# The order of short and long products on TensorE: an FNet transform ahead of a squared-ReLU layer

## The chip, the cores and the metric

The kernel runs on one core of one Trainium2 chip. The metric is the device time of one execution in microseconds, as the median of several runs.

## The reference

The input x has 8 sequences of 3008 tokens with 256 features. Each sequence goes through a two-dimensional Fourier transform, of which the real part is kept; the 24064 resulting rows go through two dense products with a squared ReLU between them.

```
X = np.fft.fft(x, axis=1)
X = np.fft.fft(X, axis=2)
x = X.real.reshape(B * S, D)        # 8 * 3008 rows, D = 256
h = x @ w_in                        # 256 -> 2048
r = np.maximum(h, 0.0)
out = (r * r) @ w_out               # 2048 -> 256
```

All is float32.

## The kernel before

**The parts.** The transform over the features is folded into w_in ahead of time (tables G1 and G2). What is left for each sequence b is a real cosine and sine transform over the tokens, in two tiles Pt and Qt for each sequence. They are made by symmetries: the rows of x are folded into sums and differences, split by even and odd frequency (kp = 0 and 1) and by cosine and sine (which = 0 and 1), so that only short products with the tables cosT and sinT remain. The highest feature of all later sequences is a case of its own, the "lone column": dft_ops(None), whose weights are 7 columns wide (one for each of the sequences 1 to 7) and not 128.

**The main loop.** The outer loop runs over steps i, each a sequence b, a block of token frequencies k0 of 252 columns (246 columns in some blocks) and a pair j of chunks of the hidden layer. In one step, TensorE (PE) does the following, in the order in which it is written:

1. `front`: four products into hP (G1 by Pt) and hQ (G2 by Qt), at line 1040. VectorE (DVE) turns them into g: two `he` instructions at line 1044 read hP, then lines 1048 and 1049 read hQ and `he`.
2. Products with w_out or with sums of its parts (wsum), for a pair of steps whose g is complete, in `run` at line 1105. They come from a fast matrix scheme: `first_half` has 12 products into the banks F, `second_half` has 8 into the banks S. Odd i has the F half, even i has the S half.

ScalarE (ACT) then does relu and square on g (lines 1053 and 1056), and GpSimd (POOL) makes the sums s of them (lines 1068 to 1085) that later products with w_out read.

**The transform beside it.** While the loop works on one sequence, the transform of the next one is laid into it piece by piece. The folding is DVE, ACT and POOL work, done by `pieces` and `first_pieces`. The products of the transform are in the two functions `even` and `odd` of each of four groups (kp, which). `even` has a product of class 0, one of class 1 (line 769) and two of `once_more` (line 867). `odd` has four of `twice_more` (line 893). These are the short products: 94 or 95 columns stream, where a product with w_out streams 164 or 168. After its four products, each function issues copies out of the bank pd on ACT (oc at lines 872 and 897, da at line 788) and then the joins on DVE (lines 804 to 821 and 905 to 929), which write Pt or Qt at the end. These functions are called through a hook: `run` calls it between two of the products with w_out. Which step gets which function is planned by `pace`, `spent` and `share`; at most one such function goes into one step.

**Banks.** hP, hQ and pd come from one pool, psh, with two buffers of the tag "h", taken in turn. In a step with a hook, hP and hQ take the two buffers and pd takes the one that hP had. The next step's hP takes that of hQ, and its hQ takes that of pd. Each instruction waits by semaphore for the last user of the buffer that it takes.

Each engine issues in the order written; tc.manual_schedule() leaves that order alone. A float32 product is two instructions on PE (two passes), and each has a weight load (PEld) of its own.

Of the kernel before, what the change touches and what calls it, by code (L numbers as in the profile page):

```python
# [84 lines left out]
def kernel(  # L85
# [111 lines left out]
    def part_of(tab, t):  # L197
        return tab[t in LATE]
# [542 lines left out]
    def dft_ops(b):  # L741
# [8 lines left out]
        def group(kp, which):  # L750
            both_in = b == 0 and which == 1
            n = NE if b is None else P
            tab = sinT if which == 1 else cosT
            n2, _, n1, n0 = NC[kp]
            st = {}

            def product(ps, c, lone_e=False, only=None):

                ts = [t for t in range(NT) if TILES[t][0] == c]
                for t in ts if only is None else ts[only:only + 1]:  # L760
                    rows = TILES[t][3]
                    if b is None:
                        w = we[0:rows, SPOT[t], kp]
                    elif lone_e:
                        w = lone[0:rows, 2 * t + kp]
                    else:
                        w = folded[b, t][0:rows, kp, PART[which]]
                        w = w[:, 0:n - both_in]
                    nc.tensor.matmul(ps[0:w.shape[-1]], w,  # L769
                                     part_of(cosT if lone_e else tab, t)[0:rows, kp, PLACE[t]:PLACE[t] + NC[kp][c]],  # L770
                                     start=t == ts[0] and (lone_e or not both_in), stop=t == ts[-1] and not lone_e,
                                     skip_group_check=both_in)
# [4 lines left out]
            def even_n():  # L777
                st["ps"] = psh.tile([P, 512], F32, name="pd", tag="h")[0:n]
                for c, at, nk in EVEN:
                    if b != 0 and c == 2:  # L780
                        st["half"] = once_more(st["ps"][:, at:], nk)
                    else:
                        product(st["ps"][:, at:at + nk], c)
                copy_4()

            def copy_4():
                a = st["a"] = hp.tile([P, -(-n2 // 16) * 16], F32, name="da", tag="da", bufs=2)[0:n]
                nc.scalar.copy(a[:, 0:n2], st["ps"][0:n, 0:n2])
# [67 lines left out]
            def once_more(ps, nk):  # L856

                nq = (nk + 2) // 2 if kp else (nk + 1) // 2
                pair = TWO, TWO + 1
                for part in range(2):  # L860
                    if kp:
                        tab, o = (cosT, sinT)[part], 0
                        to = ps[:, part * nq:part * nq + nq]
                    else:
                        tab, o = (cosT, sinT)[which], part
                        to = ps[:, part:nk:2]
                    nc.tensor.matmul(to, left(pair[part != which]),  # L867
                                     columns(tab, TWO, o)[0:HALF2], start=True, stop=True)
                if not kp:
                    return ps[:, 0:nk]  # L870
                a = hp.tile([P, NC[0][3] // 2 + 9], F32, name="oc", tag="oc", bufs=1)[0:n, 0:nq]
                nc.scalar.copy(a, ps[:, 0:nq])
                return a, ps[:, nq:2 * nq]

            def twice_more(ps):

                av, aw, bv, bw = (left(ODD0 + i) for i in range(4))  # L880
                if kp:
                    nq = (n0 + 2) // 2
                    spots = [(tab, part, ps[:, i * nq + part:(i + 1) * nq:2])
                             for i, tab in enumerate((cosT, sinT)) for part in range(2)]
                    ws = (aw, bw, bv, av) if which else (av, bv, bw, aw)
                else:
                    tab = (cosT, sinT)[which]
                    spots = [(tab, 0, ps[:, 0:n0:4]), (tab, 1, ps[:, 2:n0:4]),
                             (cosT, 0, ps[:, 1:n0 + 1:4]), (sinT, 0, ps[:, 3:n0:4])]
                    ws = (bw, aw, bv, av) if which else (av, bv, aw, bw)  # L890
                for (tab, part, to), w in zip(spots, ws):
                    cols = quarters(tab, part)
                    nc.tensor.matmul(to, w, cols[:, cols.shape[-1] - to.shape[-1]:],  # L893
                                     start=True, stop=True)
                ps_a = ps[:, 0:nq] if kp else ps[:, 5:n0 + 1:4]
                a = hp.tile([P, NC[0][3] // 2 + 9], F32, name="oc", tag="oc", bufs=1)[0:n, 0:ps_a.shape[-1]]
                nc.scalar.copy(a, ps_a)
                if kp:
                    return a, ps[:, nq:2 * nq]
                st["turned"] = a, ps_a, ps[:, 3:n0:4]  # L900
                return ps[:, 0:n0]
# [9 lines left out]
            def odd_n():  # L911
                ps = psh.tile([P, 512], F32, name="pd", tag="h")[0:n]
                st["odd"] = ps[:, 0:n0]
                st["bankodd"] = ps, 0
                st["odd"] = twice_more(ps)

            def join_odd(what, nk):

# [26 lines left out]
            if b == 0:  # L945
                named = [("copy", copy_4), ("join_4", join_4), ("join_2", join_2), ("lo", lambda: join_lo(0, NK1)),
                         ("keep", keep), ("rest", lambda: join_lo(NK1, n0)), ("hi", join_hi)]
                for e in range(2):
                    for t in range(NT):
                        c = TILES[t][0]  # L950
                        f = odd_part if c == 3 else even_part
# [1 line left out]
                        named.append((("", "e")[e] + str(t), lambda f=f, args=args: f(*args)))  # L953
                return [((which, kp, nm), f) for nm, f in named]
            def even():
                even_n()
                if kp:
                    st["bankhalf"] = st["ps"], 2 * n2
                    join_odd("half", n1)
                join_4()  # L960
                join_2()

            def odd():
                odd_n()
                if kp:
                    join_odd("odd", n0)
                else:
                    join_turned()
                join_1()
# [127 lines left out]
    def run(products, q, n, hook, end=PAIRS):  # L1097

        tb = 2 * n // 3
        begun = set()  # L1100
        for k, (nm, slot, w, v) in enumerate(products):
            if hook and k == hook[0]:
                hook[1]()
            w = wsum[:, w, q] if isinstance(w, int) else A(*w)[:, q]
            nc.tensor.matmul(acc[nm][:, slot, 0:tb], w, v, start=q == 0 and nm not in begun, stop=q == end - 1,  # L1105
                             skip_group_check=True)
            begun.add(nm)
# [176 lines left out]
    def ahead(b):  # L1284
        (_, start), *groups = dft_ops(b)
        one, two = fold_later(b)
        if b > 1:
            return one + two + [(0.0, start)] + groups
        start()
        tables = {k: (lambda tab=tab, t=t: part_table(tab, t),)  # L1290
                  for k, (tab, t) in zip((13, 14, 15, 16), ((tab, t) for t in (TWO, ODD0) for tab in (cosT, sinT)))}
        extra.update({PLAIN + 1: (take_turn, make_turn), **tables, 17: (scale_turn,),
                      **fold_columns()})
        e, (n0, m0, n1, m1, store_e) = groups[0::2], dft_ops(None)
        ready = len(one)
        composites.extend([(ready, 0, e[0]), (ready, 0, e[1]), (0, 26, n0), (0, 26, m0), (0, 26, n1), (ready, 0, e[2]),
                           (0, 26, (m1[0], lambda: (m1[1](), store_e[1]()))), (ready, 0, e[3]),
                           *((len(one + two), 0, o) for o in groups[1::2])])
        return one + two

# [121 lines left out]
    def first_pieces(i, j):  # L1422


        nonlocal drawn
        room = CAPACITY[j]
        after, since, (_, f) = composites[0] if composites else (0, per, (0.0, None))
        if drawn >= after and i >= since and (j % 2 == 0 or not side):
            composites.pop(0)
            return 2, f  # L1430
        while side and side[0][0] <= room + 0.2:
            t, f = side.pop(0)
            f()
            drawn, room = drawn + 1, room - t

    def piece_beside():

        nonlocal spent
        if side and side[0][1] in beside and spent + side[0][0] / 2 <= 0:
            t, f = side.pop(0)  # L1440
            f()
            spent += t

    ROUNDED = ['3', 'w0', '4', 'w1', '5', 'w2', '6', 'w3', '7', 'w4', 'w5', 'w6', 'w7']
    PHASES = ('TS', 'PW', 'H', 'PR', 'PU', 'PL')
# [123 lines left out]
    i = 0  # L1569
# [17 lines left out]
    for i in range(PLAIN, len(steps) + 2):  # L1587
        if i < len(steps):
            b, k0, n, j = steps[i]
# [15 lines left out]
        hook = None  # L1605
        if i < len(steps) and share(i):
            spent -= pace * share(i)
            if i < per:
                hook = first_pieces(i, j)
            else:  # L1610
                pieces()
                hook = (2, piece_beside)
        while finished and finished[0][0] <= i:
            store(*finished.pop(0)[1:])
        group = (i - 3) // 2
        at, last_half = 2 * group, i % 2 == 0
# [103 lines left out]
```

## Time and profile before

| | |
|---|---|
| median of 3 runs | 1860.83 us (1860.78 to 1861.01) |
| the profiled execution | 1860.65 us, of which the span of instructions is 1858.6 |
| PE | busy 1850.1 us, 100% of the span, 11360 passes |
| PEld | busy 1748.1 us, 94%, 11360 loads |
| DVE | busy 1474.3 us, 79% |
| POOL | busy 1461.2 us, 79% |
| ACT | busy 1075.2 us, 58% |
| mean granted TensorE clock | 1.000 |

PE and PEld are the two halves of TensorE: PE streams columns through the array, PEld loads the weights of the next pass meanwhile. The time of a pass is read from the distance of two starts; the duration that is given for one includes the way through the array, and the durations of neighbouring passes overlap. A line of the timeline gives the start, the time to the end of the last of its instructions, the engine, the line of the program, the operation, what is written and read, the shapes, how many instructions are merged in it, and in brackets the idle time before it with what ended it. A row of the list of waits reads: who waited, for whom, microseconds in total, how many times, the longest.

### The profile page before, as it was taken

What the parts mean: (1) busy time and instruction counts of PE and PEld (TensorE: products, weight loads), DVE (VectorE), ACT (ScalarE), POOL (GpSimd) and SP (SyncE); (2) the same over time, 40 slices, a digit from 0 to 9 for tenths busy, and PEclk for the clock granted to TensorE, in tenths of its full rate; (3) what the DMA queues carried; (4) which work ended last, traced back from release to release, by engine and by line L of the source; (5) the groups of instructions that cost most, each with busy time, mean ns of one, the idle gap of its engine ahead of it and who ended that gap; (6) DMA issues with size and microseconds to landing.
All of it is one profiled execution on the core that took longest, in us unless ns stands there. A gap on an engine that the chain in (4) does not pass through costs nothing.

```text
span 1858.6 us, 33954 instructions
## 1 busy us (share of the span) xinstructions
PE 1850.1 (100%) x11360; PEld 1748.1 (94%) x11360; DVE 1474.3 (79%) x3472; ACT 1075.2 (58%) x1594; POOL 1461.2 (79%) x2137
## 2 busy tenths in 40 slices
PE   9999999999999999999999999999999999999999
PEld 7699999999999999999999999999999999999998
DVE  8998878887788878778788787788878887757666
ACT  5776546565555655656456564565645666444454
POOL 4499778788788887888778887788877878787885
PEclk9999999999999999999999999999999999999999
DMA  7441101111111101111011100111001100000010
GB/s 211 109 61 41 21 21 51 41 29 23 29 34 45 26 22 32 33 46 30 15 32 46 49 15 15 46 46 35 15 21 44 37 15 21 17 21 15 21 43 23
DMA packets 153265, 69.51 MB, mean 37 GB/s; under 512 B 132577, under 2 KB 144325, under 8 KB 153092
## 3 DMA queue, kind: packets, MB, share of 16 engines
q1 hardware_dynamic: 152546, 66.80, 14.6%
q8 instruction: 91, 1.49, 0.3%
q14 instruction: 82, 0.67, 0.1%
q0 software_dynamic: 416, 0.43, 0.1%
q10 hardware_dynamic: 130, 0.12, 0.0%
HBM read 42.60 MB, written 24.69 MB: 36 GB/s over the span
## 4 chain that ended last, share of the span: by engine, by line
PE 94%; DVE 2%; POOL 1%; ACT 1%; issue 0%; DMA 0%; SPq 0%; POOLq 0%; DVEq 0%; ACTq 0%
PE F L1105 34%; PE S L1105 23%; PE hQ L1040 17%; PE hP L1040 17%; PE pd L893 1%; PE pd L867 1%; PE pd L769 1%; PE pg L351 0%; PE fin L1214 0%; DVE fd L320 0%; DVE he L1026 0%; DVE wsum L420 0%; DVE g L1029 0%; ACT g L1053 0%; PE ph L1013 0%
## 5 line engine op out<-in xcount | busy, mean ns | idle before, releaser
L1053 ACT ACTIVATE g<-g 128x1008 f32<-128x1008 f32 (+1 forms) x384 | 399.4, 1040 | 307.3 <-DVE g L1049 282.1
L1044 DVE SCALAR_TENSOR_TENSOR he<-ew,gE,hP 128x252 f32<-128x252 f32 (+1 forms) x748 | 321.2, 471 | 284.1 <-PE hP L1040 284.1
L1056 ACT ACTIVATE g<-g 128x1008 f32<-128x1008 f32 (+1 forms) x384 | 399.4, 1040 | 12.0
L1040 PE MATMUL hQ<-Qt,G 128*128 128x252 f32 (+3 forms) x1496 | 379.3, 376 | 0.6 <-ACT g L1053 0.5
L1040 PE MATMUL hP<-Pt,G 128*128 128x252 f32 (+1 forms) x1496 | 378.9, 376 | 0.0
L1105 PE MATMUL F<-s,wsum 128*128 128x168 f32 (+1 forms) x1496 | 335.5, 306 | 0.0
L1040 PEld LDWEIGHTS hQ<-Qt,G 128*128 128x128 f32 (+1 forms) x1496 | 281.6, 190 | 38.5 <-issue 2.6
L1105 PE MATMUL F<-g,wout 128*128 128x168 f32 (+1 forms) x1496 | 304.2, 305 | 0.0
L1078 POOL TENSOR_TENSOR s<-g 128x168 f32<-128x168 f32 (+1 forms) x187 | 100.8, 539 | 254.3 <-ACT g L1056 132.7
L1048 DVE TENSOR_TENSOR g<-he,hQ 128x504 f32<-128x504 f32 (+1 forms) x374 | 252.9, 676 | 41.7 <-DVE he L1044 2.7
L1040 PEld LDWEIGHTS hP<-Pt,G 128*128 128x128 f32 x1496 | 265.9, 190 | 18.8 <-issue 0.7
L1105 PE MATMUL S<-s,wout 128*128 128x168 f32 (+1 forms) x1496 | 280.7, 306 | 0.8 <-POOL s L1085 0.8
L1105 PE MATMUL S<-s,wsum 128*128 128x168 f32 (+1 forms) x1496 | 273.6, 305 | 0.0
L1105 PE MATMUL F<-g,wsum 128*128 128x168 f32 (+1 forms) x1496 | 273.6, 305 | 0.0
L1049 DVE TENSOR_TENSOR g<-he,hQ 128x504 f32<-128x504 f32 (+1 forms) x374 | 250.7, 670 | 0.0
L1105 PEld LDWEIGHTS F<-s,wsum 128*128 128x128 f32 x1496 | 247.6, 190 | 0.0
L1105 PEld LDWEIGHTS S<-s,wsum 128*128 128x128 f32 x1496 | 239.2, 190 | 8.2 <-issue 0.2
L1105 PEld LDWEIGHTS F<-g,wsum 128*128 128x128 f32 x1496 | 239.3, 190 | 8.1
L1105 PEld LDWEIGHTS F<-g,wout 128*128 128x128 f32 x1496 | 239.3, 190 | 0.0
L1105 PEld LDWEIGHTS S<-s,wout 128*128 128x128 f32 x1496 | 231.0, 190 | 1.7 <-POOL s L1085 1.0
L1081 POOL TENSOR_TENSOR s<-s 128x336 f32<-128x336 f32 (+1 forms) x187 | 168.4, 901 | 14.7
L1084 POOL TENSOR_TENSOR s<-s 128x336 f32<-128x336 f32 (+1 forms) x187 | 167.6, 896 | 14.7
(226 smaller groups left out, 2479.0 us busy)
## 6 DMA issues: line engine op xcount, KB each, us to landing
out_dram<-os SPq DMA_DIRECT2D x376, 56.0 KB
xt<-in_x_dram SPq DMA_DIRECT2D x39, 384.0 KB
xt<-in_x_dram SPq DMA_DIRECT2D x63, 128.0 KB
raw<-in_moe_w_out_dram SPq DMA_DIRECT2D x20, 256.0 KB
ew<-e_dram SPq DMA_DIRECT2D x39, 126.0 KB
out_dram<-os SPq DMA_DIRECT2D x288, 7.0 KB
raw<-in_moe_w_in_dram SPq DMA_DIRECT2D x16, 256.0 KB
xt<-in_x_dram SPq DMA_DIRECT2D x2, 512.0 KB
```

Source lines behind the costliest of these rows:

```text
L769: nc.tensor.matmul(ps[0:w.shape[-1]], w, part_of(cosT if lone_e else tab, t)[0:rows, kp, PLACE[t]:PLACE[t] + NC[kp][c]], start=t == ts[0] ...
L867: nc.tensor.matmul(to, left(pair[part != which]), columns(tab, TWO, o)[0:HALF2], start=True, stop=True)
L1040: nc.tensor.matmul(to[:, h, 0:n], w[:, fs], v[:, ks], start=h == 0, stop=True, skip_group_check=True)
L1044: nc.vector.scalar_tensor_tensor(out=t[:, h, 0:n], in0=window[b, k0][:, 0:n], scalar=gE[:, fc:fc + 1], in1=hP[:, h, 0:n], op0=ALU.mult, op ...
L1048: tt(out=g[:, :, 0:n], in0=t[:, :, 0:n], in1=hQ[:, :, 0:n], op=ALU.add)
L1049: tt(out=g[:, :, n:2 * n][:, :, ::-1], in0=t[:, :, 0:n], in1=hQ[:, :, 0:n], op=ALU.subtract)
L1053: act(g[:, :, 0:2 * n], g[:, :, 0:2 * n], AF.Relu)
L1056: act(g[:, :, 0:2 * n], g[:, :, 0:2 * n], AF.Square)
L1078: gt(out=s[:, 11], in0=b2[:, 0], in1=b1[:, 0], op=SUB)
L1081: gt(out=s[:, 4:6], in0=s[:, 4:6], in1=s[:, 10:11].to_broadcast([P, 2, tb]), op=SUB)
L1084: gt(out=s[:, 6:9:2], in0=s[:, 2:4], in1=s[:, 6:8], op=ADD)
L1105: nc.tensor.matmul(acc[nm][:, slot, 0:tb], w, v, start=q == 0 and nm not in begun, stop=q == end - 1, skip_group_check=True)
```

## The change

`even` and `odd` become generators that stop between their short products. The hook is called behind the first product with w_out of a half instead of behind the second. From then on, `run` advances the generator by one stop ahead of each product with w_out, until it is exhausted. So one short product stands between two long ones, four times in a row, and the copies and joins are issued behind the fourth as before. With L for a product with w_out and s1 to s4 for the short ones, the order on PE was L L s1 s2 s3 s4 L L ... and is now L s1 L s2 L s3 L s4 L ....

The core of the diff:

```diff
             def even_n():
                 st["ps"] = psh.tile([P, 512], F32, name="pd", tag="h")[0:n]
                 for c, at, nk in EVEN:
-                    if b != 0 and c == 2:
-                        st["half"] = once_more(st["ps"][:, at:], nk)
+                    if c == 2:
+                        st["half"] = yield from once_more(st["ps"][:, at:], nk)
                     else:
                         product(st["ps"][:, at:at + nk], c)
+                        yield
                 copy_4()
...
                 for part in range(2):
+                    if part:
+                        yield
                     if kp:
...
-                for (tab, part, to), w in zip(spots, ws):
+                for i, ((tab, part, to), w) in enumerate(zip(spots, ws)):
+                    if i:
+                        yield
                     cols = quarters(tab, part)
...
-                st["odd"] = twice_more(ps)
+                st["odd"] = yield from twice_more(ps)
...
             def even():
-                even_n()
+                yield from even_n()
...
             def odd():
-                odd_n()
+                yield from odd_n()
...
     def run(products, q, n, hook, end=PAIRS):
-        begun = set()
+        begun, short = set(), iter(())
         for k, (nm, slot, w, v) in enumerate(products):
             if hook and k == hook[0]:
-                hook[1]()
+                short = hook[1]() or short
+            next(short, None)
...
+        def last_of_e():
+            yield from m1[1]()
+            store_e[1]()
...
-            return 2, f
+            return 1, f
...
             t, f = side.pop(0)
-            f()
             spent += t
+            return f()
...
-                hook = (2, piece_beside)
+                hook = (1, piece_beside)
```

More of the change, by code (lines that the diff above doesn't have):

```diff
@@ L1295, in ahead @@
         ready = len(one)
+        def last_of_e():
+            yield from m1[1]()
+            store_e[1]()
         composites.extend([(ready, 0, e[0]), (ready, 0, e[1]), (0, 26, n0), (0, 26, m0), (0, 26, n1), (ready, 0, e[2]),
-                           (0, 26, (m1[0], lambda: (m1[1](), store_e[1]()))), (ready, 0, e[3]),
+                           (0, 26, (m1[0], last_of_e)), (ready, 0, e[3]),
                            *((len(one + two), 0, o) for o in groups[1::2])])
```

## The prediction

> **What bounds the kernel now.** I read the page's engine table first, then TensorE's own waits, then the timeline of one step, engine by engine.
>
> ```profile
> PE 1850.1 (100%) x11360; PEld 1748.1 (94%) x11360; DVE 1474.3 (79%) x3472; ACT 1075.2 (58%) x1594; POOL 1461.2 (79%) x2137
> ```
> ```profile
> PE hQ L1040 <- ACT g L1053: 0.5, 1, 0.5
> ```
>
> PE is busy all the time, and the list of its waits, of which one row stands here, adds up to 4.2 us in six waits. So the end is the sum of PE's passes: whatever makes a pass longer, or makes PE wait, is added to the time, and nothing gives it back. The next views show how near to a wait PE already is. First its weight loads around a run of four short products (each fp32 product is two passes, each with a load):
>
> ```profile
> 1617.29 0.33 PEld L1105 LDWEIGHTS S<-s,wout 128*128 128x128 f32 x2
> 1617.57 0.55 PEld L769 LDWEIGHTS pd<-sinT,w 95*128 95x128 f32 x4
> 1618.04 0.30 PEld L867 LDWEIGHTS pd<-cosT,w 94*128 94x128 f32 x2
> 1618.26 0.30 PEld L867 LDWEIGHTS pd<-sinT,w 94*128 94x128 f32 x2
> 1618.49 0.58 PEld L1105 LDWEIGHTS S<-s,wout 128*128 128x128 f32 x4
> ```
>
> Passes with w_out lie 0.139 apart (0.142 in blocks of 252 columns). The short ones lie 0.112 apart, though 95 columns stream in 0.083 (PE's rows of the lone column, four passes from 176.04 to 176.37): here the load is the limit. A load never starts before the pass ahead of it does: single rows have load and pass 1.5 ns apart beside long passes, and PEld idles 17 ns in each hP and hQ pass rather than run ahead.
>
> Then the joins on DVE, the ACT copies before them, and the next load that waits for them:
>
> ```profile
> 1616.52 0.85 DVE L1044 SCALAR_TENSOR_TENSOR he<-ew,gE,hP 128x246 f32<-128x246 f32 x2 [1.51 <-PE hP L1040]
> ...
> 1619.18 0.26 DVE L925 TENSOR_TENSOR pd<-oc,pd 128x94 f32<-128x94 f32 x1 [0.43 <-ACT da L788]
> ...
> 1620.50 0.35 DVE L805 TENSOR_TENSOR dc<-pd,db 128x188 f32<-128x188 f32 x1
> ```
> ```profile
> 1618.77 0.24 ACT L872 COPY oc<-pd 128x95 f32<-128x95 f32 x1 [3.68 <-DVE g L1049]
> 1618.90 0.24 ACT L788 COPY da<-pd 128x94 f32<-128x94 f32 x1
> ```
> ```profile
> 1620.13 0.74 PEld L1040 LDWEIGHTS hP<-Pt,G 128*128 128x128 f32 x4
> 1620.96 0.33 PEld L1040 LDWEIGHTS hQ<-Qt,G 128*128 128x128 f32 x2
> ```
>
> hP, hQ and pd share two banks (tag "h") in turn. pd takes the bank of this step's hP, so its first load waits for `he`; the next hQ takes pd's bank, so its load waits for the last join that reads pd. That join ends at 1620.84 and the load starts 0.12 later, already 0.07 behind its place (hP's fourth pass, 1620.89). It has only 0.03 left of the 0.095 by which a load (0.112) is shorter than a pass of hP (0.2075).
>
> **What the change does, and the cost of each part.** It moves only PE's order, in 60 runs: 28 even and 28 odd for sequences 1 to 7, and 4 of the lone column (7 weight columns). Before: L L s1 s2 s3 s4 L.... After: L s1 L s2 L s3 L s4 L.... s1 comes one w_out product (0.28) earlier, s4 two (0.56) later. No instruction comes or goes; DVE, ACT and POOL keep their order. The lone column's one store on SP follows its joins, off the path.
>
> *Throughput of single shorts (56 groups): taken as 0.* A slot is the longer of its stream and the next load, and the neighbours do not enter: from the first short pass to the second long one behind the run is 1.034 us, and 8 x 0.112 + 0.139 = 1.035, so going in and out of a run costs nothing. Low end: every short pass down to its stream, 448 x 0.032 = -14.3 us. High end: the first long pass behind a run is recorded 0.03 early, and were that a price, 3 more per group make +5.0. I take 0, the value of the run itself.
>
> *s1 waits for `he`.* What a load's wait for `he` looks like is in the trace already, where DVE was late:
>
> ```profile
> 479.89 0.84 DVE L1044 SCALAR_TENSOR_TENSOR he<-ew,gE,hP 128x246 f32<-128x246 f32 x2
> ```
> ```profile
> 480.79 0.41 PEld L769 LDWEIGHTS pd<-sinT,w 95*128 95x128 f32 x3
> ```
>
> The load follows `he` by 0.053, and was hidden there by 0.027 (0.139 - 0.112). At 1617, `he` ends at 1617.37, so the load can start at 1617.43; its new place is 1617.29. It is 0.14 late, 0.027 hidden: PE stands 0.11, with all w_out products queued behind it. By the same sum for a later sequence's eight groups (even and odd alternate): 0.095, 0.095, 0.10, 0, 0.28 (the case at 480), 0.11, 0.11, 0. The zeros are odd groups right behind a group that stalls in the next part, which gives `he` time. That is 0.79, times 6 sequences 4.8; sequence 1, 0.88; lone column 0.07. Sum **5.7**; 0 if something hid it, 7 if no load were hidden.
>
> *The next hQ waits for the joins.* s4 ends 4 x 0.139 = 0.556 later against everything behind it. At 1618 DVE is idle until the copies are done, so the whole chain moves by 0.556, the load has 0.03 to spare: 0.525 on PE. Only groups in the S half (8 products) with odd frequencies are tight. Per later sequence there are two, 0.49 and 0.525: 1.02, times 6 is 6.1. Sequence 1 has two even (0.48, 0.49) and two odd ones (0.58, 0.60), 2.15; the lone column two, 0.24 and 0.34. Sum **8.8**. The other S groups have their load 0.74 to 0.85 after the last join, the F groups (12 products) 0.92 to 1.18 where 0.12 is needed, which covers 0.57. If that cover were gone, 0.5 each. Relu and square stand behind the copies on ACT and POOL's sums behind those, up to 0.6 later. From the second sequence on, the last sum of a pair ends 2.4 us or more before the S products that read it, so that is hidden; in sequence 1 it may cost some tenths.
>
> *Lone column's loads are not hidden.*
>
> ```profile
> 175.52 0.33 PEld L1105 LDWEIGHTS S<-s,wout 128*128 128x128 f32 x2
> 176.04 0.26 PEld L769 LDWEIGHTS pd<-cosT,we 95*7 95x7 f32 x4 [0.18 <-issue]
> 176.29 0.34 PEld L867 LDWEIGHTS pd<-cosT,we 94*7 94x7 f32 x4
> 176.79 0.58 PEld L1105 LDWEIGHTS S<-s,wout 128*128 128x128 f32 x4 [0.16 <-issue]
> ```
>
> Between 7 and 128 weight columns the load starts only when the pass ahead has drained. Going in: 0.235 after the last long pass instead of 0.142. Going out: the first long pass streams 0.278 after the last short one instead of 0.082. Together 0.289, now once per group, then four times: 4 groups x 3 x 0.289 = **3.5** (0 if it were a cost of the run, 4.6 with a fourth).
>
> Sum: 5.7 + 8.8 + 3.5 = **18.0**. The profiled execution took 1860.65 (span 1858.6, 2.05 around it), 0.2 under the median of 1860.83. 1860.65 + 18.0 = **1878.7**. A measurement of this kernel tells apart about 0.2%, 3.7 us.
>
> **Rivals.**
> (a) *Copies start sooner.* If oc waited for its own product and not for s4, the copies (0.38) would run beside the last products; the chain would move by 0.16 to 0.21, and the 8.8 fall to 1.9: 1871.8. Against it: an even group whose da copy reads the first product's columns alone starts it only behind the fourth product, named as releaser:
>
> ```profile
> 451.38 0.24 ACT L788 COPY da<-pd 128x95 f32<-128x95 f32 x1 [2.95 <-PE pd L867]
> ```
>
> The Trainium skill, "PSUM — Partial Sum Buffer", section "PSUM bank collisions raise a hardware error", asks for guarding a bank and not an address, which is what that row shows; by it (a) would not occur.
> (b) *Loads run ahead.* If a short pass's load could be taken from an earlier long pass, each would fall to 0.08: -14.3, and with the 18.0 the end is 1864.4, no change that can be told. Against it: PEld's idle 17 ns. The Trainium skill, "TensorE: Matmul & The Clock Gate", section "Step-by-step: what each phase is for", has a 64-deep window that pulls loads ahead of running matmuls; this trace shows a depth of one.
> (c) *The other side: faster.* The same surplus, in the 448 short passes, worth 14.3, decides once the waits together cost less than 10.8 (14.3 - 3.5). With the waits at their lower ends (0 and 1.9) the sum is -14.3 + 3.5 + 1.9 = -8.9: 1851.8. For it: loads do bound the run. Against it: the row at 480 and the load at 1620.96 show both waits in force.
> (d) *It does nothing to the waits*, since PE's order hardly moves: 3.5 alone, 1864.2. Against it: the 0.03 of room.
>
> **How the numbers follow.** Forecast 0.74, own range 1873 (without the first wait) to 1885 (with the +5.0 and the tenths of sequence 1). (a) 0.10, (b) 0.07, (c) 0.06, (d) 0.03. The range of 1868 to 1885 takes in (a) with part of the first wait hidden. Slower 0.84 (forecast and a), same 0.10 (b and d), faster 0.06 (c).
>
> **What would show it.** PE's list of waits gains hQ L1040 behind DVE joins (some 16 times about 0.5) and pd L769 or L893 behind DVE `he` L1044 (some 40 times 0.1 to 0.3). Loads of single shorts still lie 0.112 before the pass that they feed; the lone column's passes show four idle stretches per group instead of one. I am wrong if short passes start 0.08 apart, if oc starts before s4 ends, or if hQ's loads keep their place.

## The result, and the profile after

The changed kernel takes 1878.63 us (median of 4 runs, 1877.79 to 1879.37) against 1860.92 in the runs beside it: a ratio of 1.0092 (95% interval 1.008 to 1.0104), so slower by 17.7 us. The forecast was 1878.7. The profiled execution has a span of 1876.3 us, 17.8 more than before, with the same 11360 passes.

The engine table and the waits of PE and of its loader, as the page and the list of waits give them:

```profile
PE 1864.0 (99%) x11360; PEld 1748.0 (93%) x11360; DVE 1474.6 (79%) x3472; ACT 1074.2 (57%) x1594; POOL 1460.8 (78%) x2137
```
```profile
PE hQ L1045 <- DVE dc L806: 3.6, 14, 0.3
...
PE hQ L1045 <- DVE Pt L806: 0.3, 1, 0.3
```
```profile
PEld hQ L1045 <- issue: 13.4, 27, 0.7
...
PEld pd L769 <- DVE he L1049: 2.1, 9, 0.3
...
PEld pd L898 <- DVE he L1049: 0.7, 3, 0.2
```

The loader's list before the change has this row, and none for pd behind `he`:

```profile
PEld hQ L1040 <- issue: 2.6, 9, 0.3
```

PE's busy time rose by 13.9 us with no more passes, while the other engines kept theirs. So the loss sits at PE, partly as idle time and partly inside recorded passes. The list of PE's waits has only 3.9 us of hQ behind DVE; the loader's rows show more (13.4 us before hQ with no releaser found, against 2.6 before the change).

The place of the loss is clearer in one step, the same as before the change. First the loads of an even run of the last sequence, now singly:

```profile
1634.06 0.40 PEld L1111 LDWEIGHTS S<-s,wsum 128*128 128x128 f32 x2
1634.54 0.30 PEld L769 LDWEIGHTS pd<-sinT,w 95*128 95x128 f32 x2
1634.76 0.30 PEld L1111 LDWEIGHTS S<-s,wout 128*128 128x128 f32 x2
1635.01 0.33 PEld L769 LDWEIGHTS pd<-sinT,w 94*128 94x128 f32 x2
1635.26 0.30 PEld L1111 LDWEIGHTS S<-s,wout 128*128 128x128 f32 x2
```

A long product and a short one, four passes, take 0.50 us from load to load (1634.76 to 1635.26), where 2 x 0.139 + 2 x 0.112 is 0.502: being single neither helps nor hurts. But the first short load comes at 1634.54, 0.48 after the first load with w_out, where one pass of hQ (0.208) and one with w_out (0.139) would have put it at 1634.41. What it waited for, and what waited in turn behind it, stands in the rows of DVE and ACT, and then of PEld again:

```profile
1633.64 0.85 DVE L1049 SCALAR_TENSOR_TENSOR he<-ew,gE,hP 128x246 f32<-128x246 f32 x2 [1.22 <-PE hP L1045]
...
1636.96 0.26 DVE L930 TENSOR_TENSOR pd<-oc,pd 128x94 f32<-128x94 f32 x1 [1.10 <-ACT da L789]
...
1638.28 0.35 DVE L806 TENSOR_TENSOR dc<-pd,db 128x188 f32<-128x188 f32 x1
```
```profile
1636.55 0.24 ACT L875 COPY oc<-pd 128x95 f32<-128x95 f32 x1 [3.79 <-PE pd L870]
```
```profile
1637.36 0.74 PEld L1045 LDWEIGHTS hP<-Pt,G 128*128 128x128 f32 x4
1638.74 0.30 PEld L1045 LDWEIGHTS hQ<-Qt,G 128*128 128x128 f32 x2 [0.64 <-issue]
```

`he` ends at 1634.49 and the load follows 0.05 later. DVE then stands idle for 1.10 us instead of 0.43 before the joins, because the copies wait for s4. The last join ends at 1638.63; hQ's load follows 0.11 later, 1.38 after hP's first load, where before the change it was 0.83.

These two distances are the same in every group that stalls, by the single records of the trace: in all 42 such groups of sequences 1 to 7 the load of s1 starts 0.052 to 0.054 behind the end of `he`, and in all 16 with an hQ wait the load of hQ starts 0.115 to 0.116 behind the end of the last join.

PE's own rows show only a part of this. First hP and hQ behind the same S half before the change, then after it:

```profile
1620.27 0.99 PE L1040 MATMUL hP<-Pt,G 128*128 128x246 f32 x4
1621.10 0.99 PE L1040 MATMUL hQ<-Qt,G 128*128 128x246 f32 x4
```
```profile
1637.49 0.99 PE L1045 MATMUL hP<-Pt,G 128*128 128x246 f32 x4
1638.77 1.07 PE L1045 MATMUL hQ<-Qt,G 128*128 128x246 f32 x4 [0.28 <-DVE dc L806]
```

Of the 0.52 us that this stretch grew by, 0.28 is idle. 0.16 lies under the last pass of hP, whose recorded duration (0.371) is that much longer than its place (0.2075), and 0.08 lies in the first pass of hQ, which is recorded as begun while its load runs.

To split the 17.8 us I compared the two traces half by half: from the first w_out pass of each of the 372 halves to the next hP, and from there to the next half. The stretches with short products grew by 9.16 us, those of hP and hQ behind them by 8.69; all the rest of the span together changed by -0.1.

| part | forecast | trace |
|---|---|---|
| single placement where nothing waits (14 groups behind a stall) | 0 | 0.005 each |
| s1 waits for `he`, sequences 1 to 7 (42 of 56 groups) | 5.6 | 5.57, the 0.005s included |
| lone column: drains, and its s1 | 3.5 | 3.59 |
| hQ waits for joins, sequences 1 to 7 (16 groups) | 8.25 | 8.09 |
| hQ waits for joins, lone column | 0.58 | 0.60 |

### The profile page after: what moved, and what is told of

Read it like the earlier page. It is cut to its first block, busy times and chain, and to the rows that moved or that the text cites. A ratio compares the mean times of both kernels' runs of the same rounds, so it can differ in the third digit from the quotient of the medians.

```text
span 1876.3 us, 33954 instructions
## 1 busy us (share of the span) xinstructions
PE 1864.0 (99%) x11360; PEld 1748.0 (93%) x11360; DVE 1474.6 (79%) x3472; ACT 1074.2 (57%) x1594; POOL 1460.8 (78%) x2137
## 3 DMA queue, kind: packets, MB, share of 16 engines
q8 instruction: 91, 1.49, 0.3%
## 4 chain that ended last, share of the span: by engine, by line
PE 92%; DVE 3%; POOL 1%; ACT 1%; issue 1%; DMA 0%; SPq 0%; DVEq 0%; POOLq 0%; ACTq 0%
PE F L1111 33%; PE S L1111 22%; PE hQ L1045 17%; PE hP L1045 16%; PE pd L898 1%; PE pd L769 1%; PE pd L870 1%; DVE fd L320 0%; PE pg L351 0%; PE fin L1220 0%; DVE wsum L420 0%; DVE he L1031 0%; DVE dc L805 0%; DVE g L1034 0%; DVE pd L930 0%
## 5 line engine op out<-in xcount | busy, mean ns | idle before, releaser
L1045 PEld LDWEIGHTS hQ<-Qt,G 128*128 128x128 f32 (+1 forms) x1496 | 280.5, 190 | 48.2 <-issue 13.4
L1111 PE MATMUL S<-s,wout 128*128 128x168 f32 (+1 forms) x1496 | 288.8, 308 | 0.8 <-POOL s L1090 0.8
L1111 PE MATMUL F<-g,wsum 128*128 128x168 f32 (+1 forms) x1496 | 278.5, 306 | 0.0
```

Source lines behind the costliest of these rows:

```text
L1045: nc.tensor.matmul(to[:, h, 0:n], w[:, fs], v[:, ks], start=h == 0, stop=True, skip_group_check=True)
```

## The experiments

The theory is that of the forecast: single placement costs nothing by itself; the places of s1 and s4 cost two waits; narrow weights cost a drain. The rivals: the price is one of single placement (each entrance costs), or loads that could run ahead bring something back. All experiments rest on one small edit of the changed kernel: a table says how many short products `run` issues ahead of w_out product k, one table each for the F halves, the S halves and the lone column. The change itself is {1:1, 2:1, 3:1, 4:1} in all three, the kernel before {2:4}.

```diff
+        plan = LONE if hook and hook[0] == 0 else F_PLAN if len(products) == 12 else S_PLAN
...
-            if hook and k == hook[0]:
+            if hook and k == 1:
                 short = hook[1]() or short
-            next(short, None)
+            for _ in range(plan.get(k, 0)):
+                next(short, None)
```

**Single placement without its waits.**

```diff
+    F_PLAN, S_PLAN, LONE = {2:1, 3:1, 4:1, 5:1}, {2:4}, {2:4}
```

> Only the 28 runs in the F halves are broken up, and only from behind the second w_out product on (L L s1 L s2 L s3 L s4): s1 keeps its place, so there is no new wait for `he`, and the F halves have room for s4's three products of delay (0.83 us against 0.9 to 1.1). All S halves and the lone column keep runs of four. This is single placement without its waits. Theory (a slot is the longer of its stream and the next load): 28 groups at 0.005 us at most, +0.1 us, 1861.0. Rival, loads run ahead: 28 x 8 passes x 0.032 = -7.2 us, 1853.7. Rival, every entrance has a price of 0.03: 28 x 3 x 0.03 = +2.5, 1863.4.

Measured: 1861.24 against 1861.16, ratio 1.0001 (0.9992 to 1.001). In the trace 26 F stretches hold short products, not 28 as expected (the S halves hold the other 30 of sequences 1 to 7), and each is 0.004 to 0.006 longer, 0.14 us in all. The loads of one of them:

```profile
1624.98 0.33 PEld L898 LDWEIGHTS pd<-cosT,w 94*128 94x128 f32 x2
1625.23 0.30 PEld L1115 LDWEIGHTS F<-s,wsum 128*128 128x128 f32 x2
1625.48 0.33 PEld L898 LDWEIGHTS pd<-cosT,w 94*128 94x128 f32 x2
1625.73 0.30 PEld L1115 LDWEIGHTS F<-g,wout 128*128 128x128 f32 x2
```

A short and a long product take 0.50 us together again (1624.98 to 1625.48). With 26 groups the rivals come to -6.7 and +2.3 us. Both lie outside the interval (-1.5 to +1.9 us), and the trace has neither: they fall. A short pass between long ones costs what it costs in a run.

**The wait of s1 alone.**

```diff
+    F_PLAN, S_PLAN, LONE = {1:4}, {1:4}, {2:4}
```

> Runs of four everywhere but one w_out product earlier (L s1 s2 s3 s4 L); the lone column as before the change. This is the wait of s1 for `he` alone: s4 ends 0.28 us sooner, so no hQ waits for joins. Theory: later sequences 0.095, 0.095, 0.10, 0.10, 0.28, 0.11, 0.11, 0.11 = 1.0 a sequence, 6.0; sequence 1 about 1.1; +7.1 us, 1868.0, with the loss in the stretch of w_out products and none between hP and the next run. The odd groups behind an even group of odd frequency, which lost nothing in the changed kernel, lose 0.1 here. Rival, the loss in those stretches is a price of single placement and not of the place: no change, 1860.9.

Measured: 1867.77, ratio 1.0036 (1.0022 to 1.0049), +6.6 us where +7.1 was expected. In the trace the stretches with short products grew by 6.79 us and those of hP and hQ shrank by 0.06 (the two small stalls of the kernel before went). The odd groups behind even ones of odd frequency lost 0.10 each, as forecast. Where `he` is late, the releaser is named:

```profile
482.22 0.84 DVE L1049 SCALAR_TENSOR_TENSOR he<-ew,gE,hP 128x246 f32<-128x246 f32 x2
```
```profile
483.11 0.52 PEld L769 LDWEIGHTS pd<-sinT,w 95*128 95x128 f32 x4 [0.25 <-DVE he L1049]
```

Nothing here is placed singly, so the loss is one of s1's place.

**The place of s4, by one step and by three.**

```diff
+    F_PLAN, S_PLAN, LONE = {2:2, 3:2}, {2:2, 3:2}, {2:4}
```

> Two and two from behind the second w_out product on (L L s1 s2 L s3 s4 L); the lone column as before the change. s1 keeps its place and s4 ends one w_out product (0.28 us) later. Theory: no wait of s1; the tight groups pay 0.28 less the room that they had: 0.20 and 0.25 in each later sequence, 6 x 0.45 = 2.7; sequence 1 0.20, 0.21, 0.30, 0.31 = 1.0; +3.7 us, 1864.6, all of it between hP and hQ of the next step. Rival, the hQ wait has another cause than s4's place: 0.

Measured: 1864.72, ratio 1.0021 (1.0011 to 1.003), +3.6 us. Between hP and the next half 3.60 us came in: 0.20 and 0.24 per later sequence; elsewhere 0.1.

```diff
+    F_PLAN, S_PLAN, LONE = {2:1, 3:1, 4:1, 5:1}, {2:1, 3:1, 4:1, 5:1}, {2:4}
```

> Singly from behind the second w_out product on in both halves (L L s1 L s2 L s3 L s4); the lone column as before the change. s1 keeps its place, s4 ends three w_out products (0.83 to 0.85 us) later. Theory: no wait of s1; each tight group pays 0.85 or 0.83 less its room: 0.77 and 0.80 in a later sequence, 6 x 1.57 = 9.4; sequence 1 0.76, 0.77, 0.86, 0.87 = 3.3; the even groups of even frequency reach the end of their room of 0.83 and pay 0.02 at most. +12.8 us, 1874.0. Rival, PE could use the later place to hide loads: -14.3 on top, 1859.7.

Measured: 1874.53, ratio 1.0073 (1.0059 to 1.0087), +13.4 us; 13.17 us behind hP, 0.77 and 0.80 per tight group. The forecast was 0.6 short. The even groups of even frequency at about 480 us and its like in the later sequences paid 0.07 where I had expected 0.02 at most (the others of that kind paid 0.02 to 0.03), and single placement cost 0.005 in each of the 56 groups, 0.29 in all, which I had left out. With the change itself in the middle, a tight group of a later sequence pays 0.24, 0.52 and 0.80 for one, two and three w_out products of delay: a straight line with a step of 0.28, two passes.

**The chain behind s4 cut short.**

```diff
                 if kp:
-                    st["bankhalf"] = st["ps"], 2 * n2
-                    join_odd("half", n1)
+                    a, _ = st["half"]
+                    nq = a.shape[-1]
+                    st["half"] = st["ps"][:, 2 * n2:2 * n2 + 2 * nq + 2].rearrange("p (o m) -> p m o", o=2)[:, 0:nq - 1]
```

> The change with the two DVE joins of the inner halves (lines 930 and 932 of the even functions of odd frequency) left out, so the values of those columns are not the reference's. The chain from s4 to the last join that reads pd becomes some 0.6 us shorter; the order on PE is that of the change. Theory: the hQ waits behind the even groups of odd frequency go (6 x 1.0, 0.95 in sequence 1, 0.22 in the lone column: -7.2); the 13 odd groups behind them, which lost 0.005 each, now lose about 0.1 at s1 (+1.3), because the hQ wait no longer gives `he` its time. 17.8 - 7.2 + 1.3 = +11.9 us over the kernel before, 1872.9. Rival, those waits come from PE's own order or from the copies: nothing changes, 1878.6. Rival, the zeros of those odd groups are their own: 17.8 - 7.2 = +10.6, 1871.6.

Measured: 1872.54, ratio 1.0062 (1.0048 to 1.0076), +11.4 us. hQ's loads keep their place behind the even groups:

```profile
1631.92 0.74 PEld L1046 LDWEIGHTS hP<-Pt,G 128*128 128x128 f32 x4
1632.71 0.58 PEld L1046 LDWEIGHTS hQ<-Qt,G 128*128 128x128 f32 x3
```

0.79 from load to load instead of 1.38. The stretches of hP and hQ lost only 1.49 us in place of 8.69, what is left being the odd groups in S halves of sequence 1 and the lone column. And the odd groups that had lost 0.005 in the changed kernel now lose 0.10 to 0.11 at s1. So the hQ wait is DVE's chain, and it had hidden the other wait in the run behind it.

**The lone column.**

```diff
+    F_PLAN, S_PLAN, LONE = {1:1, 2:1, 3:1, 4:1}, {1:1, 2:1, 3:1, 4:1}, {2:4}
```

> The change, but the four groups of the lone column (7 weight columns) go back to runs of four at their old place. Theory: the three further drains of each group (0.289 each) and its hQ waits (0.6 in all) go: 17.8 - 3.5 - 0.6 = +13.7 us over the kernel before, 1874.6; the stretches of those four groups are back at their old length. Rival, the drain is a cost of the run and not of each way in and out: nothing changes against the changed kernel, 1878.6.

Measured: 1874.75, ratio 1.0073 (1.0059 to 1.0087), +13.6 us. The four stretches are back at the length of the kernel before (within 0.003), as are those of hP and hQ behind them.

Its drains can also be taken away where they are, by wider weights.

```diff
+    we, flat = wide[:, 0:NL], wide.rearrange("p t k e -> p (t k e)")
+    WIDE = 16 * NE
+
+    def lone_w(rows, t, kp):
+        at = (2 * SPOT[t] + kp) * NE
+        return flat[0:rows, at:at + WIDE]
...
-            n = NE if b is None else P
+            n = WIDE if b is None else P
...
-                        w = we[0:rows, SPOT[t], kp]
+                        w = lone_w(rows, t, kp)
```

> The change, with the lone column's weights read 112 columns wide instead of 7 (the other 105 columns are neighbouring numbers; their rows of the result are not used). Theory: the drains come from the width of the weights: with 112 columns loads are hidden again, a short pass takes 0.10 to 0.112 instead of 0.083, and the four groups fall from 0.88 us over the kernel before to 0, or 0.05 to 0.1 below it (8 x 0.112 = 0.90 against 0.95). Their hQ waits stay. 17.8 - 3.5 - 0.2 = +14.1 us, 1875.0. Rival, the drain comes from another property of these products (their rows, or the bank): nothing changes, 1878.6.

Measured: 1876.39, ratio 1.0083 (1.0069 to 1.0097): 15.2 us over the kernel before, where I had expected 14.1 and the change itself has 17.7. The drains are gone: the four stretches are 0.04 to 0.11 over the kernel before instead of 0.88 to 0.91. But hQ behind them now waits 1.27 us instead of 0.60, and s1 waits for `he` (its load follows `he` by 0.053 in all four): the drains had covered part of both waits. What a step gives back goes in part to the next wait.

**Wider weights in the kernel before**, with runs of four at the old place and WIDE of 16, 13, 14 and 5 times 7 columns.

> The kernel before (runs of four behind the second w_out product), with the lone column's weights read 112 columns wide. Theory: each of the four groups gains the one drain pair (0.289) and pays 8 x 0.02 to 0.03 for its wider loads: -0.05 to -0.1 us each, -0.2 to -0.5 us in all, 1860.7, which shows in the trace and not in the time. Rival, the drain is no matter of width: the groups keep their 0.95 us or become longer.

Measured: 1860.53 against 1861.16, ratio 0.9997 (0.9988 to 1.0006); 0.15 off each of the four stretches in the trace, 0.59 us in all, somewhat more than expected. The time itself does not tell the two apart.

> The kernel before with the lone column's weights read 91 columns wide. The drain beside 7-column weights is gone at 112 columns; this asks where it begins. If the array counts weights by strips of 32 columns, 91 columns fill three of the four strips and a load beside 128-column weights still waits for the drain: the four stretches stay near the kernel before (2.66 us) or 8 x 0.01 = 0.1 longer. If only narrow weights drain, they shorten by 0.15 or more, as with 112 columns.

> The same with 98 columns, which reach into the fourth strip of 32. If strips of 32 decide, there is no drain and the four stretches are 0.15 to 0.25 us shorter than in the kernel before. If equal or nearly equal width is needed, they are like those with 91 columns.

Each of these widths was run once and is read from its trace. Measured from the first product with w_out to the next hP, as everywhere here, a stretch of the kernel before is 3.23 us; the 2.66 of the expectations starts behind the first two products. With 91 columns each stretch is 0.26 shorter, with 98 columns 0.23. So strips of 32 do not decide: 91 columns fill three strips and do not drain. Here are its loads, from the timed run below:

```profile
175.91 0.33 PEld L1123 LDWEIGHTS S<-s,wout 128*128 128x128 f32 x2
176.20 0.47 PEld L777 LDWEIGHTS pd<-cosT,we 95*91 95x91 f32 x4
176.59 0.41 PEld L878 LDWEIGHTS pd<-cosT,we 94*91 94x91 f32 x4
176.92 0.58 PEld L1123 LDWEIGHTS S<-s,wout 128*128 128x128 f32 x4
```

No idle time stands at either end.

> The same with 35 columns (two strips of 32). If only weights within one strip drain, the four stretches are 0.26 shorter as with 91; if a drain belongs to every width below some share of the array between 35 and 91 columns, they stay at the 2.66 us of the kernel before.

With 35 columns the stretches are 0.02 longer than before, and the loader stands idle for 0.19 us going in, against 0.18 with 7:

```profile
176.84 0.31 PEld L777 LDWEIGHTS pd<-cosT,we 95*35 95x35 f32 x4 [0.19 <-issue]
```

Where between 35 and 91 columns the drain ends, and why, stays open.

> The kernel before with 91 weight columns in the lone column, timed: the four stretches are 0.26 us shorter each in its trace, 1.04 in all, so 1860.1 against 1861.1, ratio 0.9994, less than a measurement here tells apart; if the time follows the trace, the ratio lies between 0.999 and 1.

Measured: 1859.88 against 1861.18, ratio 0.9994 (0.9984 to 1.0003). The trace has the 1.05 us in the four stretches, and the median agrees, but the interval takes in no change. It has the lowest median of the versions that were run more than once, by an amount that these runs cannot vouch for.

## Why the prediction was right

- **Throughput of single shorts, 0.** Right: 0.005 per group in 14 stretches of the change and in 26 of the F experiment. The load behind a short pass takes 0.112 whether a short or a long pass follows.
- **s1 waits for `he`.** Right in size (5.6 forecast, 5.57 found) and in pattern, the zeros behind a stall among them; the early runs of four and the shortened joins show both halves of that. (0.79 times 6 is 4.74, which stands as 4.8 in the working; the sum of 5.7 is made with 4.74.)
- **The next hQ waits for the joins.** Right (8.8, found 8.69). The three steps of delay and the shortened chain show that it is the end of s4 and the chain behind it. Rival (a), copies that start sooner, falls: oc starts 0.04 behind the recorded end of s4, with PE's pd as releaser, though it reads only what the third product wrote, which by the record was complete 0.5 us earlier. The tenths that POOL's sums might cost in sequence 1 did not come: PE's wait for s is 0.8 us before and after.
- **Lone column's drains.** Right (3.5, found 3.59, of which 0.08 is s1's wait for `he` in three of the four groups). The experiments with wider weights show that it is the narrow weights; what the load waits for there is not shown.
- **Rivals (b) and (c)**, loads that run ahead, fall with the F experiment. No load of any run, these two kernels included, started before the pass ahead of its own did. The Trainium skill's page "TensorE: Matmul & The Clock Gate", section "Step-by-step: what each phase is for", describes a 64-deep window that pulls loads ahead of running matmuls; here it brought no more than that one pass. **(d)** falls with the 18 groups whose hQ waited by 0.2 to 0.6.
- **What would show it** was right in part. The two waits were to appear in PE's own list, some 16 times about 0.5 and some 40 times 0.1 to 0.3. The list has the 16 waits of hQ, 15 behind DVE and one put down to ACT's g (0.4, though the load follows the last join there too), but at 0.2 to 0.4 each. It has no row for pd; the loader's list has pd behind `he` 12 times. The loads of a single short product start 0.14 and 0.08 before the passes that they feed, not 0.112, which is the distance from the second of these loads to the next one.
- **One sign of being wrong appeared**, short passes 0.08 apart, and it was ill chosen. The two passes of a single short product are recorded 0.085 apart (1635.148 and 1635.233), as the first two of a run of four were before the change. But the first pass of the long product behind them is recorded 0.110 later and lasts 0.03 longer: it is recorded while its load still runs. The loads themselves and the length of the stretch show 0.112. So a single start says little where a load is the limit; the distance between starts over a whole stretch holds.

## What to carry to other kernels

Before a block of work on the bottleneck engine is broken up, look at what its first instruction waits for and who waits for its last: breaking it up moves both ends. Here the first product was within 0.2 us of a wait in all 56 groups of sequences 1 to 7 (the early runs of four lost 0.08 or more in each) and the last within about 0.1 us in 16, while the list of the engine's waits had no row for either. A load that bounds a short pass is not hidden by longer neighbours when loads are only one pass ahead. The loss of one wait may hide another, so terms are to be added in the order of time and not each for itself.

## What the runs showed of the hardware that I had not expected

- A stall at a weight load is mostly not idle time of PE in the profile. Of 17.8 us more, 13.9 appear as busy time, and the list of PE's waits names 3.9 of hQ behind DVE. Part of a stall lies under the recorded duration of the pass ahead, part in the waiting pass: the short pass at 1634.54 lasts 0.347 where one that does not wait lasts 0.247, and PE has no idle time there at all. The distance between starts over a whole stretch is the measure.
- Weights of 7 or 35 columns beside weights of 128 hold the load back. Beside long passes a load of 128 columns starts 0.002 behind the start of the pass ahead of it, one of 7 columns only 0.233 behind, which is 0.09 after that pass has streamed (0.142), and on the way out the load is 0.09 late again. That this is the drain of the pass ahead is my reading; the trace names no releaser. Weights of 91, 98 and 112 columns show no such gap. With 91 columns passes start 0.080 to 0.086 apart, as with 7, though 84 more columns are loaded than are needed.
